# Loads held back one behind another, and two products split by head pair, at the start of a chunk-attention and two-layer kernel

## The chip, the cores and the metric

One NeuronCore of a Trainium2 chip. The metric is the device time of one execution in microseconds; several executions of the kernel before were timed, and one more was profiled. Engines are named as in the profile: PE (TensorE, with PEld for its weight loads), DVE (VectorE), ACT (ScalarE), POOL (GpSimd), SP (SyncE).

## The reference

```python
# q, k, v: (4, 8, 768, 64); mem_k, mem_v: (4, 8, 8, 64); chunk 32, left 16, right 8
for c in range(nc):
    k_full = concat([mem_k, k[l_start:r_end]])        # 8 memory rows, then up to 56 of the context
    a = softmax(scale * q_c @ k_full.T)
    out[c] = a @ v_full
x = out.transpose(0, 2, 1, 3).reshape(3072, 512)
h = x @ w_in;   x = (h * tanh(softplus(h))) @ w_out    # 512 -> 2048 -> 512
h = x @ w_in2;  out = (h * sigmoid(1.702 * h)) @ w_out2
```

The weights arrive as float64; the attention's inputs are float32.

## The kernel before

The 3072 tokens are cut into 8 blocks of 384. For each block the attention of 8 heads (4 head pairs, `hp`) makes the block's input x, and 16 products (`f` = 0 to 15, `forward`, line 1151) multiply it with 128 columns each of the first weight. While PE multiplies for block j, the attention of block j + 1 is fitted in between. What comes behind those blocks (the other weights, products with fewer multiplications from sums of blocks) is not touched.

**Block 0 is made in another way than the rest.** `first_pair` (line 760) loads q and k of one head pair with one DMA each, q from ACT's queue and k from SP's, turns them with PE against an identity, and ACT or DVE copies the result out of PSUM. `first_memory` (739) does the same for mem_k, `first_values` (723) loads v, in two tiles `vt` of two groups of 96 queries, from POOL's queue. Each head pair then has two quads (`gp` 0 and 1; tiles `e` and `ev`): scores (848), the masked minimum on DVE (862), four exponentials on ACT (877), the inverse of the sums on DVE (824, 827), the division (896 on DVE or 904 on ACT), the turning on PE (923), its copy `z` (929 on ACT, 930 on DVE), the product with v (940) and the copy into x (975 on ACT, 977 on DVE; tile `xh`). Block 0's products are plain float32 ones; all later ones use three products of float32r halves.

**Block 1 on** (`pair_of_heads`, 647; `values_of`, 698; `duo`, 991): q, k and v come in pieces of 32 rows, so q and k in packets of 128 bytes and v in packets of 256; DVE turns q and k (679, 682), two head pairs share one softmax.

**Weights.** `w_conv` (403) loads 128 columns as 32-bit word pairs (512 KB, tiles `wi`) and makes float32 of them in four steps: a drop of the low bits (423 on ACT, 426 on DVE), a shift (432), the low bits (436), the sign (440), the last three on DVE. The result is in the tiles `wo`, two columns blocks `f` to a tile. `w_cut` then splits each into two float32r halves for the later blocks (536 and 541). A load of block 0's weight waits until the conversion of the one six before it has begun (`pace_by`, line 407).

**What sets the order.** Every operation is put down with a rank and with costs per engine, and `Plan.issue` (207) lists them at build time: on each engine, of those that are ready by its costs, the one with the lowest rank is next. The five instruction streams so made are fixed; on the chip each engine runs its stream in that order and waits at an instruction for what it needs. A load is one entry on the queue of the engine that issues it. `opened` (line 1114) is such an entry: POOL copies one element of the second v tile, so what reads `opened` (block 1's v) stands behind it on POOL.

Of the kernel before, what the change touches and what calls it, by code (L numbers as in the profile page):

```python
# [9 lines left out]
F32 = mybir.dt.float32  # L10
# [7 lines left out]
NEG = -3.0e38  # L18
WARM = 11
# [291 lines left out]
def kernel(  # L311
# [65 lines left out]
    def load(rank, buf, parts, nbytes, run, reads=(), via=0, on=None):  # L377

        for part in parts:
            def go(queue, part=part):  # L380
                o, i = part()
                queue.dma_start(out=o, in_=i)  # L382

            way = ("sp", 0.475, lambda go=go: go(nc.sync), bus(nbytes / len(parts), run))
            if via:
                way = ("pool", via, lambda go=go: go(nc.gpsimd), bus(nbytes / len(parts), run, True))
            if on == "act":
                way = ("act", 0.5, lambda go=go: go(nc.scalar), bus(nbytes / len(parts), run))
            add(rank, [way], reads=reads, writes=[buf])
# [3 lines left out]

    w_src = {
# [8 lines left out]
    def w_conv(layer, f, part, rank, after, v, st):  # L403
# [3 lines left out]
        pace_by = begun[-1 - AHEAD:-AHEAD] if (layer, part) == (1, 0) else [pace[rank - AHEADW]] if rank < L1 else []  # L407
# [195 lines left out]
    x0, mem_t, pace, started, opened = {}, {}, {}, [], []  # L603
# [43 lines left out]
    def pair_of_heads(j, hp, rank):  # L647
# [29 lines left out]
        load(rank - (LEAD if j == 1 and hp < 2 else 4), ql, qs, P * TB * 4, 128, passed(j, rank - AHEADK), via=NARROW * (j > 1))  # L677
        load(rank - (LEAD if j == 1 and hp < 2 else 4), kl, ks, P * NKB * 128, 128, passed(j, rank - AHEADK))
# [19 lines left out]
    def values_of(j, h0, rank):  # L698
# [21 lines left out]
        load(rank, vt, parts, P * NCH * D * 4, 256, opened if j == 1 else passed(j, rank - AHEADV), via=NARROW)  # L720
        return vt

    def first_values(gp, rank):
# [3 lines left out]
        for i in range(2):  # L727
# [4 lines left out]
            )], WIN * H * D * 4, 256, via=WIDE)  # L732
        for i in range(2):
            load(rank + 0.1, vt, [lambda i=i: (
                vt[WIN:P, i], rows(mem_v, 0, [(1, NM), (NM, H)], 0, D)
            )], 0.05 * WIN * H * D * 4, 256, via=NARROW)
# [23 lines left out]
    def first_pair(hp, rank):  # L760
# [11 lines left out]
        )], 2 * TB * D * 4, 1024, on="act")  # L772
        load(rank - 4, kl, [lambda: (
# [138 lines left out]
    def quad_out(j, hp, gp, vt, rank, names, e):  # L912
# [56 lines left out]
        for hh in range(1 if apart else 2):  # L969
# [17 lines left out]
            )  # L987
            if j:
# [96 lines left out]
    def quads():  # L1085

        last, todo = None, []
        for j in range(NB):
# [17 lines left out]
            for n in range(NQ):  # L1106
                rank = base + 2 * n
                if j == 0:
                    hp, gp = divmod(n, GB // 2)
                    if n == 0:  # L1110
                        first_memory(base - 6)
                        junk = sb.tile([P, 1], F32, name="junk")
# [5 lines left out]
                    if gp == 0:  # L1118
# [32 lines left out]
    def forward(j, f):  # L1151
# [20 lines left out]
        grain = KD // 2 if j else KD  # L1172
        for k0 in range(0, KD, grain):
# [4 lines left out]
                reads=[*xs, *ws1], writes=[*done, h],  # L1178
# [492 lines left out]
```

## Time and profile before

| | |
|---|---|
| runs of the kernel before | 1097.88, 1098.87, 1102.31 us; median 1098.87 |
| the profiled execution | 1095.65 us, of which the span of the instructions is 1093.9 us |
| busy, share of the span | PE 1075.9 us (98%), PEld 95%, DVE 73%, ACT 49%, POOL 15% |
| PE busy in the 40 slices of 27.3 us | tenths 6, 8, then 9 to the end |
| PE's granted clock in those slices | 0.8, 0.7, then 0.9 or more |
| the chain that ended last | PE 90%, DMA 5%, DVE 4%, issue 1% |

A slice's digit is the busy share in tenths, 9 standing for 90% or more; the granted clock is the share of full speed that PE was given. PE is the bound nearly everywhere; the first two slices are where it is not.

### The profile page before, as it was taken

To read this page: it belongs to the slowest core of one execution; us is meant where nothing else is said; L and a number is where in the kernel's file an instruction comes from. 1 tells how busy PE (TensorE), PEld (TensorE's weight loads), DVE (VectorE), ACT (ScalarE), POOL (GpSimd) and SP (SyncE) were. 2 spreads that over 40 slices of the span, in tenths; PEclk is the share of its full clock that TensorE was granted. 3 is DMA by queue.
4 is the path that set the end of the run, shared out by engine and by line. 5 is a ranking of instruction groups with operands and counts; after the bars stand their busy time and mean duration, and the time that the engine had idled before them with its cause. 6 is when DMAs were issued, how large, how long until landed. Compare 5 with 4: busy or idle time off the path is not lost.

```text
span 1093.9 us, 25367 instructions
## 1 busy us (share of the span) xinstructions
PE 1075.9 (98%) x9936; PEld 1039.9 (95%) x9936; DVE 799.5 (73%) x1430; ACT 539.3 (49%) x1209; POOL 163.9 (15%) x273
## 2 busy tenths in 40 slices
PE   6899999999999999999999999999999999999998
PEld 5568999999999999999999999999999999999998
DVE  4896566766677689889869867666657877877875
ACT  4763544544545354555454656565565533323332
POOL 5339347537500000000000000000000000000000
PEclk8799999999999999999999999999999999999999
DMA  9998989989988573573453776868678545355361
GB/s 182 225 249 214 256 256 265 211 244 275 251 268 277 182 233 117 181 245 123 160 173 100 223 251 226 297 216 291 217 256 268 155 121 160 107 146 139 103 167 46
DMA packets 238800, 220.83 MB, mean 202 GB/s; under 512 B 70105, under 2 KB 211997, under 8 KB 238681
## 3 DMA queue, kind: packets, MB, share of 16 engines
q1 hardware_dynamic: 227865, 202.22, 62.6%
q0 software_dynamic: 9984, 16.21, 6.8%
q8 instruction: 78, 1.28, 0.5%
q10 hardware_dynamic: 832, 0.79, 0.3%
q14 instruction: 41, 0.34, 0.1%
HBM read 137.85 MB, written 81.26 MB: 200 GB/s over the span
## 4 chain that ended last, share of the span: by engine, by line
PE 90%; DMA 5%; DVE 4%; issue 1%; ACT 0%; SPq 0%; DVEq 0%; ACTq 0%
PE o L1166 12%; PE h L1166 12%; PE h L1328 9%; PE o L1429 9%; PE o L1521 9%; PE o L1328 8%; PE h L1429 6%; PE s L1429 6%; PE h L1521 6%; PE s L1521 5%; PE s L1328 4%; PE s L1065 1%; DMA wo<-in_q_dram 1%; DMA wi<-in_moe_w_in_dram 1%; PE s L1003 1%
## 5 line engine op out<-in xcount | busy, mean ns | idle before, releaser
L1166 PE MATMUL h<-xh,wi 128*128 128x384 f32 x320 | 83.7, 343 | 0.0
L1166 PE MATMUL o<-xh,wi 128*128 128x384 f32 x320 | 82.8, 340 | 0.0
L1166 PEld LDWEIGHTS o<-xh,wi 128*128 128x128 f32 x320 | 57.1, 188 | 0.6
L1166 PEld LDWEIGHTS h<-xh,wi 128*128 128x128 f32 x320 | 56.9, 188 | 0.6
L1166 PE MATMUL h<-xl,wi 128*128 128x384 f32 x160 | 53.9, 337 | 0.0
L1166 PE MATMUL o<-xl,wi 128*128 128x384 f32 x160 | 53.8, 336 | 0.0
L382 POOL DMA_DIRECT2D vt<-in_v_dram x62 | 41.0, 666 | 30.8 <-PE o L940 14.0
L1298 ACT ACTIVATE e<-h 128x384 f32<-128x384 f32 (+2 forms) x47 | 22.4, 477 | 45.5 <-PE h L1521 28.5
L1511 DVE TENSOR_TENSOR xl<-vt,xh 128x1024 fp32r<-128x1024 f32 x24 | 29.4, 1223 | 20.1 <-ACT xh L1508 18.0
L1521 PE MATMUL o<-wo,xh 128*128 128x256 f32 x232 | 43.7, 282 | 0.0
L1511 DVE TENSOR_TENSOR xl<-wi,xh 128x1024 fp32r<-128x1024 f32 x32 | 38.8, 1221 | 6.6 <-ACT xh L1508 5.9
L1429 PE MATMUL o<-xh,wo 128*128 128x256 f32 x224 | 40.7, 282 | 0.0
L382 POOL DMA_DIRECT2D wo<-in_q_dram x48 | 30.4, 639 | 45.7 <-DMA g1d<-z 16.9
L382 POOL DMA_DIRECT2D wo<-in_v_dram x56 | 35.9, 646 | 5.4 <-DMA wo<-in_q_dram 2.1
L1412 DVE TENSOR_TENSOR xl<-z,xh 128x1024 fp32r<-128x1024 f32 x24 | 29.2, 1223 | 10.2 <-ACT xh L1408 9.4
L1166 PE MATMUL h<-wo,wi 128*128 128x384 f32 x192 | 36.2, 341 | 0.0
L1521 PEld LDWEIGHTS o<-wo,xh 128*128 128x128 f32 x232 | 35.8, 190 | 0.0
L1166 PE MATMUL o<-wo,wi 128*128 128x384 f32 x192 | 35.8, 340 | 0.0
L1508 ACT ACTIVATE xh<-wi 128x1024 fp32r<-128x1024 f32 x25 | 26.4, 1054 | 18.5 <-DMA wi<-gd 8.9
L1298 ACT ACTIVATE ev<-o 128x384 f32<-128x384 f32 (+2 forms) x31 | 14.6, 471 | 42.1 <-PE o L1521 17.9
L1429 PEld LDWEIGHTS o<-xh,wo 128*128 128x128 f32 x224 | 34.8, 191 | 0.0
L1025 ACT ACTIVATE e<-s,mx 128x64 f32<-128x64 f32 x84 | 25.1, 319 | 18.1 <-DVE mx L1020 18.1
(442 smaller groups left out, 3538.8 us busy)
## 6 DMA issues: line engine op xcount, KB each, us to landing
st<-in_moe_w_out_dram SPq DMA_DIRECT2D x32, 512.0 KB
st<-wd SPq DMA_DIRECT2D x29, 512.0 KB
z<-g1d SPq DMA_DIRECT2D x24, 512.0 KB
vt<-gd SPq DMA_DIRECT2D x24, 512.0 KB
wi<-gd SPq DMA_DIRECT2D x24, 512.0 KB
g1d<-gl SPq DMA_DIRECT2D x46, 192.0 KB
g1d<-z SPq DMA_DIRECT2D x45, 192.0 KB
wi<-in_moe_w_in_dram SPq DMA_DIRECT2D x16, 512.0 KB
```

The costliest lines, as they stand in the source:

```text
L382: queue.dma_start(out=o, in_=i)
L1003: nc.tensor.matmul(out=s[hh][c0:c0 + CHUNK, g, i], lhsT=qT[d, c * CHUNK:(c + 1) * CHUNK], rhs=keys[d, c * BLK:c * BLK + KEYS], start=True, ...
L1025: nc.scalar.activation(out=e[:, g, i], in_=s[hh][:, g, i], func=AF.Exp, scale=scale, bias=mx[:, g, i:i + 1], accum_out=sm[:, g, i:i + 1],)
L1065: nc.tensor.matmul(out=o[i][hh * D:(hh + 1) * D, cs], lhsT=vt[hh][d, c], rhs=aT[hh][d, cs], start=True, stop=True, tile_position=(i * D, h ...
L1166: nc.tensor.matmul(out=h.get(), lhsT=a[:, c], rhs=b.at(kk), start=(n == 0), stop=(n == KD * len(prods) - 1))
L1298: ("act", act(n, True), lambda: nc.scalar.activation(out=dst(), in_=bank.get(), func=AF.Copy)),
L1328: nc.tensor.matmul(out=bank.get(), lhsT=a, rhs=b, start=(fresh and m == 0), stop=(m == 3 * K2 - 1), skip_group_check=not fresh,)
L1412: add(rank + 0.05, [("dve", dve(n2), lambda gh=gh, gl=gl, src=src: nc.vector.tensor_tensor(out=flat(gl), in0=flat(src), in1=flat(gh), op=A ...
L1429: nc.tensor.matmul(out=bank[:, d, :], lhsT=a, rhs=b[:, p, :], start=(fresh and h == d == p == m == 0), stop=(h == 1 and p == HP - 1 and m ...
L1508: ("act", act(NP * P), lambda: nc.scalar.activation(out=flat(gh), in_=flat(src), func=AF.Copy)),
L1511: add(rank + 0.05, [("dve", dve(NP * P), lambda: nc.vector.tensor_tensor(out=flat(gl), in0=flat(src), in1=flat(gh), op=ALU.subtract))], re ...
L1521: nc.tensor.matmul(out=bank.get(), lhsT=a[:, p], rhs=b, start=(fresh and p == 0 and m == 0), stop=(p == NP - 1 and m == 2), skip_group_che ...
```

## The change

- SP's queue now has block 0's first k ahead of mem_k.
- POOL copies one element of block 0's first k (line 1120 of the kernel after) before it issues the loads of v.
- The copy of one element of v that stood ahead of block 1's v stays.
- SP issues a DMA of one element of v (`mark`, line 1130), and the list puts the loads of the first six weight tiles and of block 1's q and k behind it.
- The products f = 0 and f = 1 of block 0 are four entries each (one per head pair) in place of one; each of the first three waits only for its head pair's two copies into x.
- The planner's cost of an early load from POOL is another one (`rank > -12`), which changes the list alone.

```diff
+SPLIT = 2
@@ load
-                way = ("pool", via, lambda go=go: go(nc.gpsimd), bus(nbytes / len(parts), run, True))
+                way = ("pool", via, lambda go=go: go(nc.gpsimd), bus(nbytes / len(parts), run, rank > -12))
@@
+    behind = []
@@ w_conv
-        pace_by = begun[-1 - AHEAD:-AHEAD] if (layer, part) == (1, 0) else [pace[rank - AHEADW]] if rank < L1 else []
+        pace_by = begun[-1 - AHEAD:-AHEAD] or behind if (layer, part) == (1, 0) else [pace[rank - AHEADW]] if rank < L1 else []
@@ pair_of_heads: q, and k in the same way
-        load(rank - (LEAD if j == 1 and hp < 2 else 4), ql, qs, P * TB * 4, 128, passed(j, rank - AHEADK), via=NARROW * (j > 1))
+        load(rank - (LEAD if j == 1 and hp < 2 else 4), ql, qs, P * TB * 4, 128, behind if j == 1 else passed(j, rank - AHEADK), via=NARROW * (j > 1))
@@ values_of
-        load(rank, vt, parts, P * NCH * D * 4, 256, opened if j == 1 else passed(j, rank - AHEADV), via=NARROW)
+        load(rank, vt, parts, P * NCH * D * 4, 256, opened[1:2] if j == 1 else passed(j, rank - AHEADV), via=NARROW)
@@ first_values: both loads
-            )], WIN * H * D * 4, 256, via=WIDE)
+            )], WIN * H * D * 4, 256, opened[:1], via=WIDE)
@@ first_pair
+        given.append((ql, kl))
@@ quad_out
+            if j == 0:
+                fresh.setdefault(hp, []).append(part)
@@ quads, at block 0's first quad
-                        first_memory(base - 6)
-                        junk = sb.tile([P, 1], F32, name="junk")
+                        first_memory(base - 3.95)
+                        junk, mark = (sb.tile([P, 1], F32, name=x) for x in ("junk", "mark"))
+                        qT, kT, done = first_pair(0, rank)
+                        opened.append(fixed())
+                        add(base - 2, [("pool", 0.15, lambda: nc.gpsimd.tensor_copy(
+                            out=junk[32:33], in_=given[0][1][32:33, 0, 0, :1]
+                        ))], reads=[given[0][1]], writes=[opened[-1]])
...
+                        behind.append(fixed())
+                        add(base + 0.5, [("sp", 0.475, lambda: nc.sync.dma_start(
+                            out=mark[:1], in_=vals0[1][:1, 1, 0, :1]
+                        ))], reads=[vals0[1]], writes=[behind[-1]])
@@ forward
-        grain = KD // 2 if j else KD
+        grain = KD // 2 if j else 1 if f < SPLIT else KD
...
-                reads=[*xs, *ws1], writes=[*done, h],
+                reads=[*(xs if j or done else fresh[k0]), *ws1], writes=[*done, h],
```

The five streams differ from those before only in their first part (on PE in some 400 rows out of 5640, the last of them among the first products of block 1); from there on they are the same, row for row. Three places show how they moved. The line numbers of the kernel after are 1 to 14 higher than those before.

ACT, from the exponentials of block 0's first head pair (`e`, `ev`) on; `wo_291<-wi_118` is the drop of the first weight tile. Before:

```order
L877 ACTIVATE e,sm<-e,mx 96x128 x4
L877 ACTIVATE ev,sm<-ev,mx 96x128 x4
L423 ACTIVATE wo_291<-wi_118 128x512
L877 ACTIVATE e,sm<-e,mx 96x128 x4
L929 ACTIVATE z_325<-o_318 128x384
L877 ACTIVATE ev,sm<-ev,mx 96x128 x3
L975 ACTIVATE xh<-o_332 128x192
```

After:

```order
L880 ACTIVATE e,sm<-e,mx 96x128 x4
L880 ACTIVATE ev,sm<-ev,mx 96x128 x4
L907 ACTIVATE e<-e,r 96x128 x4
L880 ACTIVATE e,sm<-e,mx 96x128 x4
L880 ACTIVATE ev,sm<-ev,mx 96x128 x4
L809 ACTIVATE wi_155<-h 128x120 x2
L978 ACTIVATE xh<-o_326 128x192
```

No drop of a weight stands between ACT's exponentials any more; the first two drops are on DVE, behind the masked minima of the last head pair, and a division has come to ACT.

SP's queue from the start; `wi_118` and `wi_120` (after: `wi_336`, `wi_347`) are the first two weight tiles, `wo_123` and `z_137` (after: `wo_362`, `z_131`) q and k of block 1. Before:

```order
L382 DMA w<-in_mem_k_dram 64x64
L382 DMA wi_89<-in_k_dram 100x2x256
L382 DMA wi_91<-in_k_dram 104x2x256
L382 DMA wi_109<-in_k_dram 104x2x256
L382 DMA wi_113<-in_k_dram 104x2x256
L382 DMA wi_118<-in_moe_w_in_dram 128x4x256
L382 DMA wi_120<-in_moe_w_in_dram 128x4x256
L382 DMA wo_123<-in_q_dram 32x12x32 x4
```

After:

```order
L383 DMA wi_88<-in_k_dram 100x2x256
L383 DMA w<-in_mem_k_dram 64x64
L383 DMA wi_91<-in_k_dram 104x2x256
L383 DMA wi_110<-in_k_dram 104x2x256
L383 DMA wi_113<-in_k_dram 104x2x256
L1129 DMA mark<-vt 1x1
L383 DMA wi_336<-in_moe_w_in_dram 128x4x256
L383 DMA wi_347<-in_moe_w_in_dram 128x4x256
L383 DMA wo_362<-in_q_dram 32x12x32 x4
```

The order of the loads is the same but for mem_k; what is new is the one-element DMA, at which SP stands until v is there, with everything below it waiting behind.

PE, from the last products with v of block 0 (`o<-z,vt`) on; `h<-xh,wo` are the products f = 0 and f = 1. Before (the scores of block 1, 48 rows of `s_534` and `o_536`, stand ahead of the first row):

```order
L940 MATMUL o_593<-z_325,vt 64x96 x4
L923 MATMUL o_615<-ident,e 128x96 x4
L940 MATMUL o_633<-z_325,vt 64x96 x4
L923 MATMUL o_645<-ident,ev 128x96 x4
L940 MATMUL o_662<-z_325,vt 64x96 x4
L1166 MATMUL h<-xh,wo_291 128x384 x4
L1045 MATMUL s_715<-ident,e 128x128 x3
L1166 MATMUL h<-xh,wo_291 128x384 x4
```

After:

```order
L943 MATMUL o_518<-z_303,vt 64x96 x4
L1180 MATMUL h<-xh,wo_480 128x384 x2
L926 MATMUL o_544<-ident,e 128x96 x4
L1180 MATMUL h<-xh,wo_480 128x384
L943 MATMUL o_560<-z_303,vt 64x96 x4
L926 MATMUL o_567<-ident,ev 128x96 x4
L943 MATMUL o_583<-z_303,vt 64x96 x4
L1180 MATMUL h<-xh,wo_480 128x384 x4
...
L1008 MATMUL s_616<-wo_581 32x64
L1008 MATMUL o_618<-wo_581 32x64
L1180 MATMUL h<-xh,wo_480 128x384
L1180 MATMUL o_688<-xh,wo_614 128x384 x4
```

Three of the eight quarter products of f = 0 and f = 1 now stand among the last head pair's steps, and block 1's first scores stand behind block 0's attention, ahead of the last quarter of f = 1.

## Rows read from the trace of the kernel before

**Rows 1.** Stretches: start:end, length, busy (instructions) of PE PEld DVE ACT POOL, PE's clock, DMA share, GB/s.
```profile
0.00:2.00 2.00, 0.64 (x3) 0.64 (x4) 0.85 (x7) 0.00 (x0) 1.39 (x8) 1.00 0.06 11
6.00:14.30 8.30, 6.40 (x118) 5.65 (x120) 5.07 (x37) 4.58 (x21) 2.38 (x4) 1.00 1.07 213
14.30:19.50 5.20, 2.05 (x36) 1.57 (x32) 2.60 (x17) 0.04 (x1) 1.43 (x3) 0.85 1.02 210
19.50:37.40 17.90, 13.92 (x214) 10.84 (x215) 13.84 (x67) 15.98 (x70) 6.36 (x12) 0.69 1.17 218
37.40:42.00 4.60, 3.15 (x25) 2.14 (x23) 4.15 (x12) 4.60 (x19) 1.75 (x3) 0.50 1.12 253
42.00:45.40 3.40, 3.40 (x8) 1.89 (x7) 3.40 (x12) 3.40 (x17) 3.40 (x6) 0.51 1.12 145
140.00:1094.00 954.00, 948.65 (x8380) 939.44 (x8379) 700.37 (x1115) 460.77 (x921) 93.29 (x151) 1.00 0.66 199
```

**Rows 2.** Timeline after 14.3 us: start, us, engine, instruction, [idle before <-what ended it].
```profile
19.46 0.66 ACT L423 ACTIVATE wo<-wi 128x512 f32<-128x512 f32 x1 [5.20 <-DMA wi<-in_moe_w_in_dram]
21.69 0.17 DVE L824 TENSOR_SCALAR r<-sm 96x4 f32<-96x4 f32 x1 [4.80 <-ACT e L877]
22.14 0.91 PE L940 MATMUL o<-z,vt 128*64 128x96 f32 x8 [4.16 <-POOL wo L686]
```

**Rows 3.** Timeline: end of block 0's attention, f = 0, block 1's second scores, f = 8.
```profile
37.17 0.33 ACT L975 ACTIVATE xh<-o 128x192 f32<-128x192 f32 x1
...
42.00 3.50 PE L1166 MATMUL h<-xh,wo 128*128 128x384 f32 x5
...
42.11 0.36 DVE L977 COPY xh<-o 128x192 f32<-128x192 f32 x1
...
61.68 0.24 PE L1003 MATMUL s<-z 64*32 64x64 f32 x1
...
62.85 5.43 PE L1166 MATMUL o<-xh,wo 128*128 128x384 f32 x16
68.12 2.74 PE L1166 MATMUL h<-xh,wo 128*128 128x384 f32 x8
```

**Rows 4.** Groups on ACT, 19.5 to 42.4 us: busy us, mean ns, idle before.
```profile
L975 ACT ACTIVATE xh<-o 128x192 f32<-128x192 f32 x4 | 1.3, 322 | 0.9 <-PE o L940 0.9
L904 ACT ACTIVATE ev<-ev,r 96x128 f32<-96x128 f32 x4 | 1.3, 390 | 1.0 <-DVE r L827 1.0
L929 ACT ACTIVATE z<-o 128x384 f32<-128x384 f32 x2 | 0.9, 472 | 0.0
```

**Rows 5.** Groups on DVE, 42.4 to 88.9 us.
```profile
L541 DVE TENSOR_TENSOR wi<-wo,wi 128x512 fp32r<-128x512 f32 x16 | 10.3, 671 | 0.0
L440 DVE SCALAR_TENSOR_TENSOR wo<-wi,wo 128x512 int32<-128x512 int32 x14 | 9.3, 673 | 0.0
L432 DVE TENSOR_SCALAR wo<-wo 128x512 int32<-128x512 int32 x13 | 5.5, 430 | 0.0
```

**Rows 6.** DMA by stretch: 4 to 8, 0 to 18 (two lines), 18 to 32, 32 to 41.
```profile
q0 software_dynamic: 31, 0.07, 8.0%
...
DMA packets 3185, 3.42 MB, mean 190 GB/s; under 512 B 632, under 2 KB 2920, under 8 KB 3184
...
q0 software_dynamic: 448, 1.02, 29.8%
...
DMA packets 7704, 2.38 MB, mean 170 GB/s; under 512 B 6694, under 2 KB 7445, under 8 KB 7701
...
DMA packets 3889, 2.86 MB, mean 318 GB/s; under 512 B 1247, under 2 KB 3888, under 8 KB 3888
```

**Rows 7.** Block 0's v: POOL's wait for it; DMAs of `vt`, issue to landing.
```profile
18.01 0.18 POOL L1115 COPY junk<-vt 1x1 f32<-1x1 f32 x1 [9.63 <-DMA vt<-in_v_dram]
DMA to landing us min/median/max: 9.7/10.7/11.6
```

**Rows 8.** Timeline: SP's issue of block 1's first q; ACT's ninth weight drop.
```profile
6.99 11.70 SPq L382 DMA_DIRECT2D wo<-in_q_dram  x4
55.26 0.70 ACT L423 ACTIVATE wo<-wi 128x512 f32<-128x512 f32 x1 [3.21 <-DMA wi<-in_moe_w_in_dram]
```

More of the change, by code (lines that the diff above doesn't have):

```diff
@@ L601, in rows @@
         )
-    x0, mem_t, pace, started, opened = {}, {}, {}, [], []
+    x0, mem_t, pace, started, opened, given, fresh = {}, {}, {}, [], [], [], {}
     class Inputs:
@@ L676, in pair_of_heads @@
                     ))
-        load(rank - (LEAD if j == 1 and hp < 2 else 4), ql, qs, P * TB * 4, 128, passed(j, rank - AHEADK), via=NARROW * (j > 1))
-        load(rank - (LEAD if j == 1 and hp < 2 else 4), kl, ks, P * NKB * 128, 128, passed(j, rank - AHEADK))
+        load(rank - (LEAD if j == 1 and hp < 2 else 4), ql, qs, P * TB * 4, 128, behind if j == 1 else passed(j, rank - AHEADK), via=NARROW * (j > 1))
+        load(rank - (LEAD if j == 1 and hp < 2 else 4), kl, ks, P * NKB * 128, 128, behind if j == 1 else passed(j, rank - AHEADK))
         add(rank, [("dve", dve(TB), lambda: nc.vector.transpose(
@@ L735, in first_values @@
                 vt[WIN:P, i], rows(mem_v, 0, [(1, NM), (NM, H)], 0, D)
-            )], 0.05 * WIN * H * D * 4, 256, via=NARROW)
+            )], 0.05 * WIN * H * D * 4, 256, opened[:1], via=NARROW)
         return vt
@@ L1117, in quads @@
                         ))], reads=[vals0[1]], writes=[opened[-1]])
-                    if gp == 0:
+                        behind.append(fixed())
+                        add(base + 0.5, [("sp", 0.475, lambda: nc.sync.dma_start(
+                            out=mark[:1], in_=vals0[1][:1, 1, 0, :1]
+                        ))], reads=[vals0[1]], writes=[behind[-1]])
+                    elif gp == 0:
                         qT, kT, done = first_pair(hp, rank)
```

## The prediction

> **What bounds the kernel now.** I read the busy time by stretch first. From 140 us on PE is busy 948.65 of 954 us at full clock [rows 1], and that part of the five streams is the same after the change. So the change can only move the moment at which this dense stretch begins. What it can win is bounded too: between 14.3 and 42.0 us PE is idle 5.20-2.05 + 17.90-13.92 + 4.60-3.15 = 8.6 us, and from 37.4 to 45.4 us its clock is at 0.5 (1.2 instead of 2.4 GHz) while it is busy 3.15 + 3.40 us [rows 1], half of which, 3.3 us, full clock would give back.
>
> Then the timeline, for what PE waits for. ACT has done its first eight exponentials at 19.46 - 5.20 = 14.26 us and then stands before the drop of the first weight tile, which has not landed. DVE waits 4.80 us for ACT's exponentials, and PE 4.16 us for the chain behind them [rows 2]; the profile names a POOL copy there, but POOL's copy feeds block 1. The reader should see one wait three times: an instruction that nobody needs for 20 us stands in ACT's queue ahead of work that all wait for. After it ACT is nearly full, 15.98 of 17.90 us, DVE 13.84 [rows 1], up to the last copy into x at 42.11 + 0.36 = 42.5 us [rows 3].
>
> **Part 1: ACT's stop goes.** In ACT's new order a division of four pieces stands after the eight exponentials, then the next eight exponentials. A piece costs 0.39 us [rows 4] and overlaps its neighbour a little, so the four take about 1.3 us; ACT starts on the second head pair at 14.3 + 1.3 = 15.6 us. Before, it started at 19.46 + 0.66 = 20.1 us.
>
> From there to ACT's last copy before was 37.17 + 0.33 - 20.1 = 17.4 us [rows 3], of which one drop of 0.66 [rows 2] and waits of 0.9 + 1.0 us [rows 4]; work 14.8 us. The new order adds there two copies of turned scores (2 x 0.47), three copies into x (3 x 0.32) and two first halves of a weight split, not shown in these rows, which I price as the drop of the same 128x512 (2 x 0.66 [rows 2]); one division less takes 1.3 us out again, and overlaps of 0.1 us at each of these take some 0.6: +1.3 us, work 16.1 us. ACT now also makes the last copy into x, so its end is the end of block 0's attention. For waits I take 3.7 us, twice those before, since the last quads have nothing to overlap with: 15.6 + 16.1 + 3.7 = 35.4 us. With waits of 1.0 us it would be 32.7, with 6.4 us (more than the whole stop removed) 38.1. Against 42.5 us that is **7.1 us** earlier, 4.4 to 9.8. DVE allows it: it takes over two drops and three more divisions in this stretch, and gives five copies to ACT and block 1's first maxima to later, which is about even.
>
> **Part 2: from there to f = 8.** Before, f = 8 starts at 68.12 us, 25.6 us after the end of the attention, and f = 0 had started 0.5 us ahead of that end, at 42.00 [rows 3]; so PE needs 26.1 us from f = 0 to f = 8. After, three quarters of products are done among the attention's last steps: a product takes 2.74 us [rows 3], a quarter 0.67, so 2.0 us less. Block 1's first scores, which stood ahead, now come behind the attention; the second ones took from 61.68 to 62.85 [rows 3], so 1.2 us more. And DVE: the third conversion (f = 2) can end behind those scores; before the fourth ends, DVE must do two maxima (not in these rows; half a pass over 512 columns and its start, about 0.5 each), two shifts of 0.43 and three passes of 0.67 us [rows 5], 3.9 us with some small ones, less overlaps 3.6; one product covers 2.7 of it, so PE stands 0.9 us. 26.1 - 2.0 + 1.2 + 0.9 = 26.2 us, against 25.6: **-0.6 us**. The half clock at f = 0 (to 45.4 us [rows 1]) stays in both.
>
> **Part 3: the held loads.** Holding v is priced at nothing, gain or loss: v had moved only 0.07 MB by 8 us [rows 6], so it was not in the way of the first k and q, and it is issued again while 0.7 MB of q and k are still to come. Holding the weights and block 1 costs time on the DMA engines, which are full from 2 us on (share 1.02 to 1.17 [rows 1]). Before v lands, 0.79 MB of q, 0.84 of k (from the shapes) and 1.02 of v [rows 6] must come, 2.65 MB; at the 213 GB/s of 6 to 14.3 us [rows 1] from 2 us on that is 14.4, with its end 15 us, where before it was 18.01 [rows 7]. Then SP issues the one-element DMA and the weights. At the program's start 1.3 us pass from the first issue to the first bytes (0 to 2 us: 11 GB/s [rows 1]); so bytes flow again at about 17 us, 2 us of idle DMA. By 18 us before, 3.42 MB had moved [rows 6], so 0.77 MB of weights are now still to come at 318 GB/s, 2.4 us, then the mixed loads of 18 to 32 us, 14 us for 2.38 MB [rows 6]: the stretch of pure weights that began at 32 begins at 33.4 us. All later loads are **1.4 us late**.
>
> Does PE meet that? The first weight tile is now dropped among DVE's steps for the last head pair, which I put at about 25 us, 10 ahead of the attention's end; it comes at 17 + 3, the double of 0.5 MB at full rate, with v of block 1 beside it. The ninth tile, dropped at 55.26 us before as soon as it came [rows 8], comes at 56.7; drop 0.66, shift 0.43 and two passes of 0.67 [rows 2, 5] make 59.1, with what stands ahead on DVE 60. f = 8 would start at 35.4 + 26.2 = 61.6. The lateness is covered, by 1.5 to 2 us and no more: **0**, with ends 0 and -2.
>
> DVE in the whole stretch from 42.4 to 88.9 us is the second cover; it has 16 splits of 0.67 us there [rows 5], and in the new order eight of them, not four, are done before f = 8, so it is not behind.
>
> **The sum.** 7.1 - 0.6 - 0 = 6.5 us off the profiled execution's 1095.65: 1089.15. The median of the runs is 3.22 us above that execution, so 1098.87 - 6.5 = 1092.4 us.
>
> **The rivals.** *The clock stays up.* The granted clock is 0.85, then 0.69 after the gap of 4.16 us, and 1.0 before it [rows 1, 2]. Without that gap it may hold through the attention and the first products: 3.3 us more, 6.5 + 3.3 = 9.8 off, 1089.1 us. Against it: from 37.4 to 42 us PE was busy 3.15 of 4.60 and still at 0.50. The Trainium skill (TensorE: Matmul & The Clock Gate, Part 1) says the throttled state is the default and activity releases it, which speaks for this rival; the rows agree only for the first gap. Chance 0.13.
>
> *The wait changes engine.* The drop of the first weight is now on DVE, ahead of a copy and a division of the last head pair, and on PE the first quarters stand ahead of a turning; all later loads stand behind v on SP. If v takes the 10.7 us from issue to landing that it took [rows 7], though issued at about 11 us, it lands at 22, 7 us later than I reckon: the ninth tile at 63.7, f = 8 at 66, and 2 us are left: 1096.8. For it: v's pieces are the last that landed before 18 us [rows 7]. Against: those 10.7 us were on engines shared with weights and block 1. The Trainium skill (DMA: Bandwidth & Descriptors, Rules for kernel authors) would have a DMA issued early and waited for late, so that its fixed cost overlaps, which speaks against every hold here; the 1.3 us above is such a cost, and I count it once. Chance 0.25, from no gain to 4.5 us.
>
> *Slower.* SP took 11.70 us to issue four pieces of block 1's q, since a place must come free for each [rows 8]. If the sixteen such pieces wait as long in series, on top of a v at 22 us, the loads are 7 + 11.7 us late, block 1's last k is there at 33.4 + 18.7 = 52.1, turned at 52.9, and PE, which reaches the scores (now ahead of f = 2) some 3.6 us after the attention, at 39.0, stands 13.9 us: 13.9 - 6.5 = 7.4 slower, 1106.3. It decides where the lateness passes 39.0 - 0.8 - 33.4 + 6.5 = 11.3 us. Chance 0.06.
>
> *It does not do what it says*: the drop could still stop someone. The streams exclude it for ACT; for DVE it is the second rival.
>
> **How the numbers follow.** My forecast, 4.5 to 8.5 us off, has 0.56. A measurement of this kernel can tell 0.5%, 5.5 us, from no change; my forecast's interval lies above that with some three quarters (0.43), so faster is 0.13 + 0.43 = 0.56; same 0.13 + 0.25 = 0.38; slower 0.06. The range leaves out half of the second rival's low end and the slower one, and some of the best: 1088.5 to 1098.5, that is 10.4 to 0.4 us off.
>
> **What would show it.** Right: no ACT wait for a weight between exponentials; block 0's last copy into x at 33 to 38 us; POOL's second copy at 14 to 16 us; the ninth tile's drop at 56 to 58; f = 8 at 60 to 63; after 140 us nothing new. Wrong: DVE waiting at the first drop, PE waiting for the scores or f = 2 by more than 2 us, POOL's copy at 18 us or later, or a granted clock at 0.5 past 50 us.

## The result and the profile after

The kernel after takes a median of 1104.58 us over 20 runs (1100.2 to 1106.8), the kernel before 1098.41 over 20 runs made in turn with it (1095.96 to 1102.31). The ratio is **1.0052, with a 95% interval of 1.0042 to 1.0063**: half a per cent slower, about 5.7 us. Forecast were 1092.4 us, from 1088.5 to 1098.5; "slower" was given 0.06. So the prediction was wrong in sign, and its range missed the time.

The profiled executions are 1095.65 us before and 1106.37 after: the one lies 2.8 us below its median, the other 1.8 above. Their spans differ by 10.7 us, of which some 4.5 is which execution was caught. So in the traces I compare times and places, and take sizes from the ratios.

Stretches of the kernel after (start:end, length, busy and count of PE PEld DVE ACT POOL, granted clock, DMA share, GB/s):

```profile
14.30:19.50 5.20, 4.53 (x74) 3.64 (x70) 5.20 (x33) 5.20 (x27) 2.57 (x5) 1.00 0.28 65
19.50:37.40 17.90, 15.10 (x108) 9.96 (x103) 14.69 (x55) 12.49 (x49) 8.47 (x15) 0.81 1.05 195
37.00:52.60 15.60, 12.86 (x129) 7.18 (x128) 10.72 (x28) 8.32 (x33) 4.29 (x8) 0.89 1.07 213
42.00:70.00 28.00, 22.89 (x251) 13.53 (x250) 20.20 (x46) 15.88 (x64) 11.32 (x20) 0.94 0.93 192
70.00:100.00 30.00, 22.26 (x149) 12.56 (x149) 20.62 (x43) 12.05 (x26) 9.77 (x18) 0.83 0.86 207
72.00:78.70 6.70, 1.39 (x6) 0.81 (x6) 5.36 (x15) 1.18 (x3) 0.02 (x1) 0.83 1.12 249
78.70:84.00 5.30, 5.29 (x10) 2.97 (x11) 4.59 (x10) 4.02 (x8) 0.25 (x1) 0.57 0.49 99
140.00:1094.00 954.00, 952.61 (x8427) 943.15 (x8413) 704.97 (x1130) 467.19 (x950) 93.06 (x155) 1.00 0.67 201
```

The same two long stretches, and the one in which weights moved almost alone, of the kernel before:

```profile
34.00:42.50 8.50, 7.05 (x141) 5.41 (x140) 8.00 (x28) 8.50 (x38) 2.25 (x4) 0.56 1.09 285
42.00:70.00 28.00, 28.00 (x270) 17.14 (x269) 24.98 (x57) 17.29 (x54) 11.73 (x21) 0.94 1.09 231
70.00:100.00 30.00, 29.30 (x298) 20.43 (x297) 24.68 (x60) 16.11 (x55) 21.23 (x35) 1.00 0.90 225
```

Read them in this order. The last row after is as dense as that of [rows 1]: the loss is made earlier. In 14.3 to 19.5 us the compute engines won what was forecast: ACT 5.20 of 5.20 us busy (0.04 before), PE 4.53 (2.05). But the DMA engines, full before (1.02), were at 0.28. And between 42 and 100 us PE, which had been busy 57.30 of 58 us, is busy 45.15. The seven microseconds won in front are lost behind, and more with them. Nothing of this is at the end of the program: the last product with the first weight ends at 370.7 us before and 380.6 after, and what follows takes 723.2 and 724.0 us.

The timeline of the kernel after (start, us, engine, instruction, idle before and what ended it) shows both halves:

```profile
15.02 0.39 ACT L880 ACTIVATE e<-e,mx 96x128 f32<-96x128 f32 x1
16.87 0.17 POOL L1125 COPY junk<-vt 1x1 f32<-1x1 f32 x1 [4.85 <-DMA vt<-in_v_dram]
17.59 0.97 SPq L383 DMA_DIRECT2D wi<-in_moe_w_in_dram  x2
32.93 4.25 SPq L383 DMA_DIRECT2D wi<-in_moe_w_in_dram  x6
33.91 1.28 POOL L383 DMA_DIRECT2D vt<-in_v_dram  x2 [6.50 <-PE o L926]
35.10 0.31 ACT L978 ACTIVATE xh<-o 128x192 f32<-128x192 f32 x1
45.24 4.51 PE L1180 MATMUL o<-xh,wo 128*128 128x384 f32 x8 [2.67 <-DVE wo L442]
52.62 0.66 ACT L425 ACTIVATE wo<-wi 128x512 f32<-128x512 f32 x1 [1.19 <-DMA wi<-in_moe_w_in_dram]
54.72 2.85 PE L1180 MATMUL h<-xh,wo 128*128 128x384 f32 x8 [1.73 <-DVE wo L442]
63.45 0.68 ACT L425 ACTIVATE wo<-wi 128x512 f32<-128x512 f32 x1 [1.84 <-DMA wi<-in_moe_w_in_dram]
66.53 5.40 PE L1180 MATMUL h<-xh,wo 128*128 128x384 f32 x16 [0.70 <-DVE mx L1025]
72.43 0.56 DVE L1313 COPY z<-o 128x384 f32<-128x384 f32 x1 [3.56 <-DMA g1d<-z]
74.67 0.52 PE L1050 MATMUL s<-ident,e 128*128 128x128 f32 x3 [2.75 <-DVE r L827]
78.71 7.64 PE L1180 MATMUL o<-xh,wo 128*128 128x384 f32 x16 [0.84 <-DVE wo L442]
85.01 1.03 SPq L383 DMA_DIRECT2D wi<-in_moe_w_in_dram  x2
91.88 0.67 ACT L425 ACTIVATE wo<-wi 128x512 f32<-128x512 f32 x1 [1.17 <-DMA wi<-in_moe_w_in_dram]
```

And of the kernel before, for the same loads (the ninth drop, 55.26 us, is in [rows 8]):

```profile
28.56 5.68 SPq L382 DMA_DIRECT2D wi<-in_moe_w_in_dram  x6
40.25 1.28 POOL L382 DMA_DIRECT2D vt<-in_v_dram  x2 [14.03 <-PE o L940]
43.68 0.72 ACT L423 ACTIVATE wo<-wi 128x512 f32<-128x512 f32 x1
67.06 0.38 SPq L382 DMA_DIRECT2D wi<-in_moe_w_in_dram  x1
```

The attention's last copy into x ends at 35.4 us, as forecast. But the six weights that SP issued from 28.56 us before are issued from 32.93, 4.4 us late; the eighth drop comes at 52.62, as its load lands, instead of 43.68, where ACT did not wait for the load; the ninth at 63.45 instead of 55.26, both times as its load lands; the last two loads are issued from 85.01 instead of by 67.06. PE waits for weights at 45, 55, 79 us. The lateness grows from 4 to 18 us along the way. The longest wait of PE, 2.75 us ahead of 74.67 and 1.81 more ahead of 77.00, has another start: DVE stands 3.56 us in front of a copy whose place a store of an earlier product (`g1d`, 192 KB) still holds. SP issued that store at 61.20 us among the late weights, and it took 11.2 us to land. So stores are late too, on the same DMA engines.

The bytes tell the same in one number. DMA of the first 100 us, before and then after:

```profile
DMA packets 36341, 22.08 MB, mean 221 GB/s; under 512 B 22560, under 2 KB 34545, under 8 KB 36327
```
```profile
DMA packets 34795, 19.18 MB, mean 192 GB/s; under 512 B 22195, under 2 KB 33515, under 8 KB 34782
```

**The theory** after this reading: in the kernel before, PE's work and the loads end together. The change moves the first forward and the second back, and the second decides. The rivals: the four-part products or another part of the new plan cost the time; the loads' order (the late last weights, block 1's v beside the weights) costs it, not the hold; or SP's queue limits the loads.

### The profile page after: what moved, and what is told of

It is laid out like the page before. It is cut to its first block, busy times and chain, and to the rows that moved or that the text cites. A ratio compares the mean times of both kernels' runs of the same rounds, so it can differ in the third digit from the quotient of the medians.

```text
span 1104.6 us, 25379 instructions
## 1 busy us (share of the span) xinstructions
PE 1080.2 (98%) x9936; PEld 1039.8 (94%) x9936; DVE 800.5 (72%) x1429; ACT 539.5 (49%) x1211; POOL 161.9 (15%) x273
## 4 chain that ended last, share of the span: by engine, by line
PE 87%; DMA 7%; SPq 2%; DVE 2%; issue 1%; ACT 1%; POOL 0%; DVEq 0%; ACTq 0%; POOLq 0%
PE h L1180 11%; PE o L1180 11%; PE o L1535 9%; PE o L1443 9%; PE h L1342 9%; PE o L1342 8%; PE h L1535 6%; PE h L1443 6%; PE s L1535 6%; PE s L1443 6%; PE s L1342 4%; DMA wi<-in_moe_w_in_dram 4%; SPq L383 2%; PE s L1070 1%; PE s L1008 1%
```

## The experiments

Unless it is said otherwise, a variant has each engine's instructions in the order of its base, so that one thing alone differs. Ratios are to the kernel before, run in turn on the same chip; a variant has 5 to 12 runs. The medians of the kernel before beside them lie from 1097.66 to 1098.96 us, so variants are compared by their ratios. Ratio and medians disagree most for no_mark: 1.0004, but 1100.84 us beside 1097.92.

| variant | median us | ratio [95%] |
|---|---|---|
| no_mark | 1100.84 | 1.0004 [0.9987, 1.0021] |
| no_hold | 1099.38 | 1.0002 [0.9985, 1.0019] |
| holds_only | 1105.08 | 1.0065 [1.0040, 1.0089] |
| split_only | 1101.78 | 1.0036 [1.0023, 1.0049] |
| w_free | 1101.78 | 1.0033 [1.0020, 1.0046] |
| w01_first | 1106.22 | 1.0067 [1.0046, 1.0088] |
| stop_gone | 1097.86 | 0.9998 [0.9982, 1.0014] |
| v1_late | 1102.01 | 1.0029 [1.0013, 1.0044] |
| w14_early | 1104.04 | 1.0061 [1.0047, 1.0076] |
| late_w14 | 1100.80 | 1.0026 [1.0012, 1.0039] |
| free_w14 | 1098.32 | 1.0003 [0.9993, 1.0014] |
| after_qpool | 1104.51 | 1.0051 [1.0037, 1.0065] |
| free_qpool | 1104.78 | 1.0053 [1.0037, 1.0068] |
| more_mb | 1103.26 | 1.0045 [1.0028, 1.0062] |
| less_mb | 1095.94 | 0.9981 [0.9968, 0.9994] |
| less_stop | 1095.26 | 0.9973 [0.9960, 0.9986] |
| free_late_w14 | 1096.39 | 0.9983 [0.9968, 0.9998] |

### Taking the holds away: no_mark, no_hold

```diff
 no_mark, and no_hold
-                        add(base + 0.5, [("sp", 0.475, lambda: nc.sync.dma_start(...))], reads=[vals0[1]], ...)
+                        add(base + 0.5, [("sp", 0.475, lambda: None)], reads=[vals0[1]], ...)
 no_hold alone
-                        add(base - 2, [("pool", 0.15, lambda: nc.gpsimd.tensor_copy(...))], reads=[given[0][1]], ...)
+                        add(base - 2, [("pool", 0.15, lambda: None)], reads=[given[0][1]], ...)
```

> The changed kernel without the one-element DMA on SP; every other instruction stands in the same order, v still waits for the first k. Late-loads theory (the change loses because each weight lands 8 to 20 us later than before, and the wait for v on SP is where that begins): weights are issued from about 6 us, not 17.6; the ninth weight tile is dropped at 56 us or earlier, not 63.5; f = 15 ends at 90 to 94 us, not 100; time 1092 to 1097. Order theory (what costs is the new order of PE and DVE: quarters, block 1's scores behind the attention): time stays at 1103 to 1106. Between them, 1098 to 1102, if v, sharing the DMA engines again, lands at 18 us or later and holds up block 0's attention.

> As no_mark, and POOL's copy of the first k is gone as well, so v is issued at once. Late-loads theory: v lands earlier than in no_mark, the weights about as there, time within 2 us of no_mark, 1092 to 1097. Order theory: 1103 to 1106. If the hold of v is worth something by itself (the first q and k land earlier with it), this is 1 to 3 us slower than no_mark.

Without the element of v that SP waits for, most of the loss is gone: 1.0004 instead of 1.0052. That is **5.3 us**, and some 3 to 7.5 with both intervals; by the medians 2.9 us of the loss stay, and the expected 1092 to 1097 us came neither here nor in no_hold. Its timeline: six weights are issued from 26.09 us, and the attention ends at 39.2, some 4 us later than with the hold. By 100 us 20.96 MB have moved, more than with the hold (19.18) but not the 22.08 of before.

```profile
26.09 10.32 SPq L383 DMA_DIRECT2D wi<-in_moe_w_in_dram  x6
38.87 0.31 ACT L978 ACTIVATE xh<-o 128x192 f32<-128x192 f32 x1
```

Without either hold the attention ends at 38.3 us, 4.2 earlier than before, 22.02 MB have moved by 100 us, as many as before, and the time is that of before (1.0002; free_w14 below, which has no hold either, 1.0003). So within the intervals SP's hold is the whole of the loss, and the hold of v by itself costs and gives nothing that can be seen. The new order, with an attention that ends 4 us earlier and loads on the old schedule (six weights from 29.00 us, before 28.56), wins nothing. Whether the loads use up those 4 us, as the theory has it, or the new order itself costs as much elsewhere, these two runs do not tell apart.

The Trainium skill (DMA: Bandwidth & Descriptors, Rules for kernel authors) would have a DMA issued early and waited for late, so that its fixed cost overlaps. The runs agree on issuing early: held back, the loads left the engines at a share of 0.28 for 5.2 us, and the kernel lost the 5.3 us just named. That it was a fixed cost which was lost is not shown.

### Each half of the change, planned anew: holds_only, split_only, w_free

```diff
 holds_only: after
-SPLIT = 2
+SPLIT = 0
 split_only: before, with the products f = 0 and 1 in four entries
+        grain = KD // 2 if j else 1 if f < SPLIT else KD
 w_free: after, weights not behind v
-        pace_by = begun[-1 - AHEAD:-AHEAD] or behind if (layer, part) == (1, 0) else ...
+        pace_by = begun[-1 - AHEAD:-AHEAD] if (layer, part) == (1, 0) else ...
```

> The changed kernel without its second half: the products of f = 0 and 1 whole again, both holds kept (the planner writes the orders anew). By the runs so far the hold on SP costs 5.3 us at the changed order and the quarters alone cost the kernel before 3.9. If the hold is the whole cause: 1103 to 1106, as the changed kernel. If the two costs add: 1099.5 to 1102.

> The kernel before with the second half of the change alone: the products of f = 0 and 1 done in quarters, head pair by head pair; no load held, ACT's drop of the first weight tile where it was. My forecast's part 2 gave the quarters 2.0 us; stop_gone showed that an earlier end of the attention alone gives nothing. Late-loads theory: within 1.5 us of the kernel before, 1096.5 to 1099.5. Order theory (the quarters hold up block 0's attention or wait themselves): 1100 to 1103.

> The changed kernel with only block 1's q and k held behind v, the weights free (the planner then loads twelve weight tiles ahead of block 1's first q). Idle theory: the DMA engines are never idle and move long packets first, so PE's products of block 0 run early: 1094 to 1099, level with the kernel before or better. Rival (v lands late among 6 MB of weights and holds up block 0's attention, or block 1's attention comes too late for PE): 1100 to 1108.

The holds alone are as slow as both together (the intervals overlap), so the four-part products neither cause the loss nor give anything that can be seen beside it. They are not free by themselves, though: planned into the kernel before, they lose 0.4%. There PE stands 5.44 us for a copy on ACT. That copy waited 1.50 us for a store, and in ACT's queue ahead of it stand drops of weights that waited 3.30 and 0.83 us for their loads (timeline of split_only):

```profile
65.37 0.68 ACT L424 ACTIVATE wo<-wi 128x512 f32<-128x512 f32 x1 [3.30 <-DMA wi<-in_moe_w_in_dram]
71.28 0.49 ACT L1301 ACTIVATE z<-h 128x384 f32<-128x384 f32 x1 [1.50 <-DMA g1d<-z]
71.82 5.49 PE L1169 MATMUL h<-xh,wo 128*128 128x384 f32 x8 [5.44 <-ACT z L1301]
```

So loads are late there too, without any hold: 20.50 MB have moved by 100 us. Why the new plan makes them so was not pursued. w_free, expected level with the kernel before, gives 2 us back of the 5.7, from a stream that differs in more than the hold; it decides nothing alone.

### Filling the idle gap: w01_first

The element of v is behind the first two weight loads in SP's queue, so that these fill the 5 us.

```diff
+        first = self.mark[0], self.mark[1]
+        order = [o for o in order if o not in first]
+        n = order.index(self.mark["mark"])
+        order[n:n] = first
```

> The changed kernel with the one-element DMA on SP moved behind the first two weight tiles, so that these 1 MB fill the DMA engines while SP's other loads wait for v (from 14.3 to 19.5 us they had a share of 0.28). Idle theory (what the hold costs is the DMA engines' idle time, 2.9 MB less moved by 100 us): 1 to 3.5 us faster than the changed kernel, 1101 to 1103.5. Rival (v shares the engines, lands later, and the wait for it is as long at its end): 1104 to 1106.

It gives nothing back (1.0067). 3.73 MB have moved by 19.5 us, as in the kernel before (3.78; after 2.91), but by 32 us only 5.26 (before 5.81, after 5.16): v and with it the mark came later, 20.14 us instead of 16.83, and the rest of the loads behind them (timeline of w01_first).

```profile
20.14 0.71 SPq L1138 DMA_DIRECT2D mark<-vt  x1
32.35 3.27 SPq L388 DMA_DIRECT2D wi<-in_moe_w_in_dram  x5
```

So filling the idle gap alone gives nothing back: block 1's 32 short loads and the six weights (from 32.35 us, after 32.93) still start late. Since the same edit made v later, the price of the gap by itself is not shown. Why it is a little slower than the kernel after, if it is, stays open.

### ACT's stop alone: stop_gone

The kernel before, its first two drops on ACT moved to just ahead of the first shift.

```diff
+        late = [o for o in order if name(o) == "drop_act"][:2]
+        order = [o for o in order if o not in late]
+        n = next(n for n, o in enumerate(order) if name(o) == "shift")
+        order[n:n] = late
```

> The kernel before, with one thing moved: ACT's drops of the first two weight tiles stand in its queue just before the first shift on DVE needs them; all other orders as before, no load held. My step 'ACT's stop goes' by itself: block 0's last copy into x at 36 to 38 us instead of 42.5, and if PE's order bounds from there, 4 to 6 us off: 1092 to 1095. Late-loads theory: from f = 8 on the weights bound here too (the ninth was dropped as soon as it came, at 55.26 us), so that part of the gain is lost: 1095 to 1098. If nothing is gained at all, 1098 to 1099, the loads set the start of the dense stretch in the kernel before as well.

The expected end of the attention, 36 to 38 us, did not come; by the timeline of stop_gone the last copy is at 42.38 us, where it was:

```profile
28.24 0.61 DVE L687 STREAM_TRANSPOSE wo<-wo 128x416 f32<-128x416 f32 x1 [3.27 <-DMA wo<-in_k_dram]
42.38 0.35 DVE L982 COPY xh<-o 128x192 f32<-128x192 f32 x1
```

ACT no longer stands; instead DVE stands 3.27 us in front of the turning of block 1's k, which the list has among block 0's steps and which lands only then. The stop that the profile showed was worth nothing alone: the next late load stood right behind it.

### The order of the loads: v1_late, w14_early, late_w14, free_w14

v1_late puts a POOL copy of an element of the weight tile of f = 7 (`staged[7]`, the eighth loaded) ahead of the loads of v for block 1's second four heads, so that these wait for it. w14_early moves SP's loads of the last two weights ahead of block 2's first loads. late_w14 is both; free_w14 is no_hold with the latter.

```diff
 v1_late
+            plan.ahead[plan.ops[n]] = lambda: nc.gpsimd.tensor_copy(
+                out=more_junk[0][64:65], in_=staged[7].get()[64:65, :1].bitcast(F32)
+            )
 w14_early
+        first = self.mark[14], self.mark[15]
+        order = [o for o in order if o not in first]
+        n = order.index(self.mark["mem"])
+        order[n:n] = first
```

> The changed kernel with one copy more on POOL, ahead of the loads of v for block 1's second four heads, that waits for weight tile 7 (of 0 to 15). These loads were issued from 33.9 us, beside the weight tiles 2 to 7, which then took from 37.0 to 52.6 us where the kernel before took 34.1 to 42.5. Collision theory: the weights 3 to 7 land 4 to 7 us earlier, tile 7 at 46 to 49 us, the ninth is dropped at 57 to 60 us, and the time falls by 2 to 6 us, to 1099 to 1102.5. Rival (the weights are slow because of block 1's q on the same queue, or the loads of v only move to collide with the next weights): tile 7 lands at 51 us or later, time 1103 to 1107.

> The changed kernel with SP's loads of the last two weight tiles (14 and 15 of 0 to 15) moved ahead of block 2's k and shared keys, where the kernel before had about the same place; the holds stay. In the changed kernel they were issued at 85.0 us, behind k pieces that wait for a free place, and ACT dropped tile 14 at 90.05 us. Late-loads theory: these two land before 80 us, the wait of PE ahead of f = 14 (2.34 us) goes, and the time falls by 1.5 to 3.5 us from 1104.6, to 1101 to 1103. Rival (the DMA engines are the bound, so what comes sooner for one comes later for the next: block 1's attention or tiles 12 and 13 wait instead): 1104 to 1106.

> The changed kernel with both moves, the later v of block 1's second four heads (v1_late, 2.5 us less than the changed kernel) and the early weight tiles 14 and 15, holds kept. If the two causes add: 1098 to 1100, level with the kernel before although SP still stands until v has landed. If SP's wait for v is what costs and the two only shift the shortage about: 1101 to 1103, as v1_late.

> no_hold (the changed order without either hold) with the same move of weight tiles 14 and 15 on SP. no_hold stood 2.31 us ahead of f = 14 and came out level with the kernel before. Late-loads theory: 1.5 to 3 us less than no_hold, 1095 to 1097, so a little faster than the kernel before. Rival (DMA engines as the bound): 1098 to 1099, as no_hold.

v1_late gives 2.5 us back. In the kernel after POOL could issue that v at 33.9 us instead of 40.3, since the attention gave its place free earlier; so its packets of 256 bytes ran beside the weights. The stretches above show what that did: the DMA engines are as busy in 37.0 to 52.6 us after (share 1.07) as in 34.0 to 42.5 before (1.09), but carry 213 GB/s instead of 285. The packets in the two stretches, before and then after:

```profile
DMA packets 4113, 2.42 MB, mean 285 GB/s; under 512 B 2084, under 2 KB 4074, under 8 KB 4112
```
```profile
DMA packets 4810, 3.33 MB, mean 213 GB/s; under 512 B 2331, under 2 KB 4553, under 8 KB 4809
```

About half of the packets are short in both (block 1's next q and k move in both), and the mean packet after is no smaller, some 690 bytes against 590. So the length of v's packets is not shown to be the reason for the lower rate. That v's loads are in the way of the weights is shown by holding them back. With v held the eighth tile is there at 44.26 (timeline of v1_late):

```profile
44.26 0.38 POOL L730 COPY junk<-wi 1x1 f32<-1x1 f32 x1 [17.52 <-DMA wi<-in_moe_w_in_dram]
56.62 0.68 ACT L430 ACTIVATE wo<-wi 128x512 f32<-128x512 f32 x1 [1.38 <-DMA wi<-in_moe_w_in_dram]
```

Still the ninth drop waits for its load until 56.62, and a part of the loss stays. Earlier last weights (w14_early, free_w14) change nothing. In free_w14 they come early, but at about the same place ACT now waits for a store, and PE stands 4.18 us instead of no_hold's 2.31 (timeline of free_w14):

```profile
80.49 0.49 ACT L1318 ACTIVATE z<-h 128x384 f32<-128x384 f32 x1 [6.82 <-DMA g1d<-z]
81.03 7.59 PE L1186 MATMUL h<-xh,wo 128*128 128x384 f32 x16 [4.18 <-ACT z L1318]
```

That fits the rival of both expectations, the DMA engines as the bound: what comes sooner for one transfer comes later for the next. And the wait which the expectations put ahead of f = 14 (2.34 us in the kernel after) stands ahead of f = 13, for a copy of an earlier result that ACT makes behind the drops of the last two weights.

### SP's queue: after_qpool, free_qpool

Block 1's 32 pieces of q and k from POOL's queue in place of SP's, in the kernel after and in no_hold.

```diff
-            way = ("sp", 0.475, lambda go=go: go(nc.sync), ...)
+            way = ("sp", 0.475, lambda go=go: go(queue or nc.sync), ...)
 in both loads of pair_of_heads
+        ..., queue=nc.gpsimd if j == 1 else None)
```

> The changed kernel with block 1's 32 pieces of q and k issued from POOL's queue, at their places in the planned order there, in place of SP's; both holds stay (SP waits for v, POOL's pieces stand behind its own wait for v). On SP the weight tiles 2 to 7 then follow the first two at once: issued by 24 us, not 32.9. Queue theory (the weights are late because they stand on SP behind 16 pieces that take 11 to 14 us in whatever stretch they fall): tile 7 lands by 42 us, not 52.6, the ninth is dropped by 57 us, and the time falls by 4 to 8 us, to 1097 to 1101. Engine theory (the pieces' short packets take the DMA engines' time, from whichever queue): the weights come sooner but block 1's pieces later, PE or DVE wait for those, and the time is 1102.5 to 1107.

> The same move of block 1's q and k to POOL's queue, without the two holds (the order of no_hold, which came out level with the kernel before). Queue theory: the first eight weight tiles are there by 30 us, block 0's products never wait, and the earlier end of the attention can be kept: 1092 to 1096, faster than both kernels. Engine theory: v and the first k share the engines with 4 MB of weights, block 0's attention ends at 40 us or later, block 1's q and k come after that: 1097 to 1104.

In the timeline of after_qpool SP issues eight weights early, but PE then stands before block 1's scores:

```profile
16.89 11.62 SPq L383 DMA_DIRECT2D wi<-in_moe_w_in_dram  x8
48.61 0.31 PE L1008 MATMUL s<-wo 64*32 64x64 f32 x1 [5.49 <-DVE wo L688]
```

Whichever goes first, weights or block 1's pieces, the other is late, and no_hold loses its even time by the move (1.0053). In after_qpool the DMA engines have a share of 1.02 to 1.11 from 20 to 50 us, so there they are full while SP's queue is free of the pieces; that speaks against SP's queue as the limit. free_qpool settles less, because its engines are not full (its stretches):

```profile
30.00:40.00 10.00, 6.28 (x38) 3.42 (x38) 4.88 (x13) 3.82 (x14) 7.08 (x12) 0.84 0.77 165
40.00:50.00 10.00, 8.38 (x112) 4.80 (x113) 6.19 (x17) 4.30 (x13) 10.00 (x17) 0.83 0.62 161
```

POOL issues the pieces there one after another, with waits between them from 20.34 to 64 us, so its queue may be the new limit. The Trainium skill (DMA: Bandwidth & Descriptors, Rules for kernel authors) says that spreading DMAs over queues doesn't raise the bandwidth. after_qpool agrees: with the pieces on another queue the time is the same (1.0051).

### How much cover the loads have: more_mb, less_mb, less_stop

more_mb adds two transfers of 0.5 MB to the kernel before, from a weight that is not needed yet to a scratch place in HBM. less_mb loads only half of the weight tiles f = 2 to 5, 1.05 MB less, and clears the other half on POOL (the cut in the diff holds for those four tiles and on the source too; these products are not the reference's). less_stop is less_mb with the edit of stop_gone.

```diff
 more_mb, ahead of the third weight load
+        for i in range(2):
+            nc.sync.dma_start(out=more_d[i], in_=w_src[2, 1][i * P:(i + 1) * P, :])
 less_mb
-                st.get().rearrange("p (k c) -> p k c", k=KD),
+                st.get().rearrange("p (k c) -> p k c", k=KD)[:, :KD // 2],
+            lambda: nc.gpsimd.memset(st.get()[:, DM:].bitcast(F32), 0.0)
```

> The kernel before with two more transfers of 0.5 MB each from HBM to HBM on SP's queue, just ahead of weight tile 2 (issued at about 28 us); nothing reads them. At the 303 GB/s of 32 to 42 us 1 MB is 3.5 us of the DMA engines' time. If the DMA engines set the start of the dense stretch in the kernel before too (no cover, as stop_gone suggests): 2.5 to 5 us slower, 1100.5 to 1103. If the cover of 1.5 to 2 us that I reckoned with exists: 0 to 2 us, 1098 to 1100.

> The kernel before with half of weight tiles 2 to 5 left out (1 MB less to load; the other half of each is set to zero on POOL while it waits for v, so the products of f = 2 to 5 use wrong weights; their work is the same). If the loads set the start of the dense stretch in the kernel before (1 MB more cost 4.9 us): 2.5 to 5 us faster, 1093.5 to 1096.5. If the chain of ACT, DVE and PE sets it, as I forecast: 0 to 1 us, 1097.5 to 1099.

> less_mb and stop_gone together: 1 MB less to load, and ACT's first two weight drops moved behind. If with fewer loads the attention's earlier end counts after all: 2 us or more below less_mb, 1090 to 1094. If it still gives nothing (block 1's q and k, which DVE waits for in its order, keep the attention where it is): within 1 us of less_mb.

One megabyte more costs 0.45%, **4.9 us** (3.1 to 6.8). At the 213 GB/s of [rows 1], 1.05 MB take 4.9 us, at the 303 of the expectation 3.5: estimates that leave little or no cover. One megabyte less gives 2.1 us, less than the 2.5 to 5 expected; from 42 us on PE is full then. Stretches of more_mb, and then of less_mb:

```profile
42.00:70.00 28.00, 26.17 (x258) 15.18 (x257) 16.81 (x36) 14.01 (x44) 11.63 (x21) 0.88 1.04 202
70.00:100.00 30.00, 26.42 (x264) 15.45 (x263) 28.93 (x68) 17.62 (x59) 15.65 (x26) 0.94 0.84 216
```
```profile
42.00:70.00 28.00, 28.00 (x269) 17.01 (x269) 27.08 (x64) 19.89 (x62) 11.31 (x20) 0.95 1.11 244
70.00:100.00 30.00, 30.00 (x304) 21.53 (x303) 21.99 (x51) 13.62 (x45) 23.34 (x38) 1.00 0.84 213
```

That fits the balance which the theory states: more load is paid, less load gains only until PE has no idle time left. less_stop is within 1 us of less_mb; whether an earlier attention would count once the loads are shorter stays open, since stop_gone's edit does not end the attention earlier.

### The parts put together: free_late_w14

no_hold, with the edits of v1_late and w14_early: the attention's new order, no hold for block 0, and block 1's second v behind the eighth weight tile.

> The changed order without both holds, with the later v of block 1's second four heads and the early last two weight tiles: the best parts by the runs so far. If the later v is worth here what it was in the changed kernel (2.5 us): 1095 to 1097, a little faster than the kernel before. If without the hold these loads no longer meet weight tiles 2 to 7: 1098 to 1099.5, level with it.

0.9983 [0.9968, 0.9998]: 1.9 us faster than before, just clear of no difference (and one of 17 variants, so weak evidence of a gain), and by the ratios some 7.5 us faster than the kernel after. The last two weights are dropped at 81.03 us (after: 90.05 and 91.88), and no clock is lost from 42 us on (timeline, then stretches):

```profile
81.03 1.27 ACT L439 ACTIVATE wo<-wi 128x512 f32<-128x512 f32 x2
```
```profile
42.00:70.00 28.00, 26.74 (x316) 16.26 (x299) 26.66 (x68) 18.56 (x71) 17.82 (x31) 1.00 1.11 232
70.00:100.00 30.00, 26.88 (x287) 18.86 (x286) 21.56 (x49) 15.18 (x49) 13.98 (x25) 1.00 0.87 214
```

## Why the prediction was wrong

- **What bounds the kernel: half right.** "The change can only move the moment at which this dense stretch begins" held; the moment moved the other way. That the dense stretch ahead of 140 us, 42 to 100, hung on loads that came just in time was not looked for.
- **Part 1 was right in its number, in part by luck.** Second head pair on ACT at 15.02 us (forecast 15.6), last copy into x ending at 35.4 (35.4), no wait for a weight between the exponentials. But it laid all 7.1 us to ACT's new order. With the same order and no hold the attention ends at 38.3: in these traces 4.2 us are the order's and 2.9 the holds', which bring block 0's q and k sooner (without them PE waits for a k, timeline of no_hold):

```profile
17.62 1.65 PE L783 MATMUL h<-ident,wi 104*64 104x104 f32 x16 [2.62 <-DMA wi<-in_k_dram]
```

In the kernel after the earlier end is real and brings nothing: no_hold keeps 4.2 us of it and is not faster.

- **Part 2 was right in what it counted, and short by the weights**: f = 8 at 66.53 us instead of 61.6, with waits of 2.67 and 1.73 us for conversions whose loads had come late.
- **Part 3 is the step that failed**: "All later loads are **1.4 us late** ... The lateness is covered, by 1.5 to 2 us and no more: **0**, with ends 0 and -2." The hold of v was rightly priced at nothing (1.0004 with it, 1.0002 without), and SP's own wait was near: v at 16.87 us (forecast 15), SP going on at 17.59 (17). But the lateness was carried on as a constant. It was 4.4 us at the six weights, ahead of which 16 short pieces of block 1 stand in SP's queue; 8.9 at the eighth drop, because block 1's second v, set free by the very gain of part 1, fell on the weights; 8.2 at the ninth; 18 at the last. And the cover was looked for up to f = 8 alone, from one drop; more_mb shows little or none over the whole. no_mark prices the step at 5.3 us (some 3 to 7.5), not 0.
- **The rivals.** "The wait changes engine" put the ninth tile at 63.7 us and f = 8 at 66, which is what came (63.45 and 66.53), but by luck: it has v at 22 us, which came at 16.87, and leaves out the 0.9 us of other work on DVE that part 3 counts between the same two. It also stopped counting there: 1096.8 leaves out the eight products behind. "Slower" had SP's short pieces right as what is late, and the wrong place: PE did not stand before block 1's scores but later, before weights and behind a late store. "The clock stays up" came in part: 1.00 in 37.4 to 42 us, but 0.57 in 78.7 to 84 us, after the longest wait.
- **The sum.** To the forecast's -6.5 us belongs +5.3 for the hold (no_mark), and for the gain itself nothing, with the loads where they were (no_hold). 0 + 5.3 is the 5.7 measured, within the intervals.

So what is shown: SP's hold makes the loss, all of it within the intervals (no_mark, no_hold), the loads had little or no cover (more_mb, less_mb), the earlier v takes some 2.5 us of the loss (v1_late). That the remaining part is spread over the short pieces, the later weights and the late stores is read from the traces and not shown apart.

## What to carry to other kernels

Before a delay of loads is priced at nothing, ask how much room the loads have, over the whole stretch in which they matter and not up to the next consumer: a kernel with a megabyte of load more, and one with a megabyte less, answer it in two runs. Where compute and loads end together, an earlier compute step may be worth nothing, and it frees buffers, so look which transfers start earlier through it and what they run beside. Compare two kernels by the megabytes moved up to a few moments; a DMA share near 1 says nothing of that.

## What the hardware showed that was not expected

- The busy share of the DMA engines can hide a quarter of their rate: 1.07 at 213 GB/s and 1.09 at 285, in the two stretches named under v1_late, with packets that are no shorter on average.
- The granted clock goes down late in the program's start too, where PE waits: 0.57 in 78.7 to 84 us, after PE was busy 1.39 of 6.70 us. Of its two levels, 2.4 and 1.2 GHz, 0.57 is mostly the lower. Sixteen matmuls (two products f) took 7.64 us there, 5.40 at 66.53 us. The wait here cost its own length and then 2.2 us more.
